# Cross attention and two gated layers on one core: the state reads' softmax moves into the x reads' stage, and both halves of the attention get new places

## The chip, the core and the metric

The kernel runs on one core of a Trainium2 chip: TensorE (PE) multiplies 128-row tiles into PSUM, VectorE (DVE), ScalarE (ACT) and GpSimd (POOL) work on tiles, and SyncE (SP) issues nearly all DMAs from one queue. Every engine takes its instructions in a fixed order. The metric is the device time in microseconds (us) of one execution; a version's time is the median of its runs.

## What is computed

```python
B, H, S, Ns, D = 8, 8, 512, 32, 64
a  = softmax(x @ state.T / 8)        # x reads:     [B, H, S, Ns]
a2 = softmax(state @ x.T / 8)        # state reads: [B, H, Ns, S]
attn = concat([a @ state, a2 @ x], axis=2)     # per head
t = attn.transpose(0, 2, 1, 3).reshape(8 * 544, 512)
t = (sigmoid(t @ w_gate) * (t @ w_val)) @ w_out        # d_ff 1536
out = square(relu(t @ w_in)) @ w_out2                  # d_ff 2048
```

Both softmaxes come from the same scores: `a2` is the softmax over the other axis. Everything is fp32; a product is made of three matmuls of split operands (high by high, high by low, low by high; lines 182 to 184). The weights arrive as 64-bit words that are converted on the way (`to_single`, line 108).

## The kernel before

**First part.** The gated layer's products with w_gate and w_val are taken with the state first: `state_weights` (L457) multiplies the 32 state rows of each head by a chunk of w_gate and w_val and stores the result in DRAM (`g_dram`, tile `gd`), for blocks 0 to 3 and then for 4 to 7. There are six chunks of 256 columns. The x rows of a block then need only their attention weights `a`: `front_x` makes the gate (`psg`), its sigmoid `sg`, the value (`psv`) and their product `g` (L556) from `a` and `gg`, the split form of a chunk's part `gi` that `load_g` fetched from `gd`. `back1` multiplies `g` by w_out1 into four accumulators. One front and one back are a **unit**: blocks 0 to 3 with f = 0 to 5 (units 0 to 23), again with f = 6 to 11 (24 to 47), then blocks 4 to 7 with 12 each (48 to 95). Unit 58, for one, is block 4 with f = 10: the first that needs chunk 5 for blocks 4 to 7. Units 96 to 107 are the state rows of all blocks (`front_s`): their input `xs_t` is the state reads of all eight blocks, split into high and low in `split_states`, their weights `ws` come back from DRAM (`load_gv`).

**Attention.** Block b has two groups g of four heads. Stage A (`LX, A20, A21, A3, A4`) loads x transposed, makes the scores `s2`, stores them to DRAM (`s_dram`, tile `sd`) and makes the x reads' weights `a` from their transpose `e1`, with an exponential on ScalarE (L336). Stage B (`LN, LS, B4, B5, SX, B60, B61, B7`) loads x and the scores (`e2`), takes the exponential with its sum (L359), scales by the reciprocal (L363 on ScalarE for blocks 0 to 3, else L365 on VectorE), transposes (`ps_e2`, `et`), multiplies by the split x (`xs`; `ps_sr`, `tmp`, `sw`) and turns the result into `xs_t` (`ps_so`). ScalarE holds one table of functions: between a sigmoid and an exponential stands an ACT_TABLE_LOAD.

**Beside it** w_in2 and w_out2 are converted and written back in the form of the second part (`prep_steps`: loads `raw`, tiles `c`, `wa`, `wu`, stores `wi` and `wo`).

**What sets the order.** Each stage is a closure that `spread` puts at a due time counted in units; `front_x`, `front_s` and `back1` run what is due at their six steps. From the program so written a scheduler makes the fixed order of each engine; it may move an instruction ahead of others of its engine. The small PSUM tiles of the attention, of `state_weights` and of the transposes (tag `at`) share a ring of two and get their slots in the order of the program. Where a tile's slot or its data are late, all behind it in its engine's order wait. The pools `e2`, `s2`, `xs`, `et` have one buffer each.

**Second part** (from unit 107 on): the squared-relu layer with seven products for each two by two blocks.

In the trace's names digits at a word's end are left out: `e` is `e1` or `e2`, `s` is `s2`, `ps_s` is `ps_s2`.

Of the kernel before, what the change touches and what calls it, by code (L numbers as in the profile page):

```python
# [32 lines left out]
def kernel(  # L33
# [247 lines left out]

    def group_stages(b, g):

        v = {}
# [37 lines left out]

        def a4():
# [22 lines left out]
            nc.vector.tensor_sub(out=a[:, 1, g, :], in0=a1, in1=a[:, 0, g, :].bitcast(F32))  # L346

        def ls():
            v["e2"] = f_p.tile([P, S], F32, tag="e2", name="e2", bufs=1)
            nc.sync.dma_start(out=v["e2"], in_=s_dram[b, g])  # L350

        def b4():

            s2 = v.pop("e2")
            nm = sm_p.tile([P, 1], F32, tag="nm", name="nm")
            sm = sm_p.tile([P, 1], F32, tag="sum", name="sum")
            nc.vector.tensor_reduce(out=nm, in_=s2, axis=AX.X, op=ALU.max, negate=True)
            nc.vector.tensor_scalar_mul(nm, nm, scale)
            nc.scalar.activation(out=s2, in_=s2, func=AF.Exp, bias=nm, scale=scale, accum_out=sm)  # L359
            nc.vector.tensor_scalar_add(sm, sm, 1e-9)  # L360
            nc.vector.reciprocal(out=sm, in_=sm)
# [80 lines left out]
    def attention(b):
        gs = [group_stages(b, g) for g in range(2)]
        pick = lambda names: [
            (lambda: None) if n == "-" else gs[int(n[-1])][n[:-2]] for n in names
        ]
        return [lambda: prep_diag(b), *pick(ORDER_A)], pick(ORDER_B)
# [114 lines left out]
    def split_states():  # L562
        t = two["sp"].tile([P, 2, KD, NSTATE], F32R, name="sp")
        nc.scalar.copy(out=t[:, 0], in_=xs_t)
        nc.vector.tensor_sub(out=t[:, 1], in0=xs_t, in1=t[:, 0].bitcast(F32))
        s_parts["a"] = t
# [543 lines left out]
```

## Time and profile before

| | us |
|---|---|
| median of 3 runs (1497.92 to 1499.72) | 1499.65 |
| the profiled execution's own time | 1500.54 |
| its span, first to last instruction | 1498.8 |
| PE busy | 1431.0 (95%) |
| DVE, ACT, POOL busy | 940.2, 748.8, 246.0 |
| DMA | 311.68 MB, mean 208 GB/s |

A matmul's record is longer than its share of a busy PE, since matmuls overlap; the number of matmuls in a window tells more than the busy time. The first part, with attention, takes about the first 790 us, the second the rest.

### The profile page before, as it was taken

To read this page: it belongs to the slowest core of one execution; us is meant where nothing else is said; L and a number is where in the kernel's file an instruction comes from. 1 tells how busy PE (TensorE), PEld (TensorE's weight loads), DVE (VectorE), ACT (ScalarE), POOL (GpSimd) and SP (SyncE) were. 2 spreads that over 40 slices of the span, in tenths; PEclk is the share of its full clock that TensorE was granted. 3 is DMA by queue.
4 is the path that set the end of the run, shared out by engine and by line. 5 is a ranking of instruction groups with operands and counts; after the bars stand their busy time and mean duration, and the time that the engine had idled before them with its cause. 6 is when DMAs were issued, how large, how long until landed. Compare 5 with 4: busy or idle time off the path is not lost.

```text
span 1498.8 us, 19379 instructions
## 1 busy us (share of the span) xinstructions
PE 1431.0 (95%) x6552; PEld 1176.9 (79%) x6552; DVE 940.2 (63%) x1579; ACT 748.8 (50%) x1291; POOL 246.0 (16%) x216
## 2 busy tenths in 40 slices
PE   5879999999999989999899999999999999999998
PEld 3558878887787677888798788888888888888887
DVE  7986887578889987555536655734575356433443
ACT  6865876456678887666424522332242223232211
POOL 1112213232344544333101100000000000000000
PEclk9889999999999999999999999999999999999999
DMA  9984799699999864333677844644365443645442
GB/s 265 341 263 120 229 328 339 210 363 292 323 296 286 254 211 145 95 113 92 242 271 250 274 158 147 217 146 143 133 227 188 151 152 134 222 124 195 155 145 80
DMA packets 244595, 311.68 MB, mean 208 GB/s; under 512 B 105361, under 2 KB 152977, under 8 KB 244497
## 3 DMA queue, kind: packets, MB, share of 16 engines
q1 hardware_dynamic: 242224, 309.66, 63.8%
q10 hardware_dynamic: 2272, 0.79, 0.3%
q8 instruction: 52, 0.85, 0.2%
q14 instruction: 47, 0.38, 0.1%
HBM read 221.25 MB, written 89.13 MB: 207 GB/s over the span
## 4 chain that ended last, share of the span: by engine, by line
PE 72%; DVE 10%; ACT 7%; DMA 7%; issue 3%; SPq 1%; POOL 0%; ACTq 0%; DVEq 0%; POOLq 0%
PE o L182 8%; PE o L183 8%; PE o L184 8%; PE px L183 4%; PE px L182 4%; PE px L184 4%; PE acc L183 4%; PE acc L184 3%; PE acc L182 3%; DMA raw<-in_moe_w_out_dram 2%; PE psg L182 2%; PE psg L183 2%; PE psg L184 2%; PE psv L182 2%; PE psv L183 2%
## 5 line engine op out<-in xcount | busy, mean ns | idle before, releaser
L182 PE MATMUL o<-wo,g2h 128*128 128x512 f32 x512 | 198.6, 390 | 3.7 <-DMA wo<-wo 3.0
L183 PE MATMUL o<-wo,g2h 128*128 128x512 f32 x512 | 199.1, 389 | 0.0
L184 PE MATMUL o<-wo,g2l 128*128 128x512 f32 x512 | 193.9, 389 | 0.0
L537 POOL TENSOR_TENSOR gg<-gi,gg 128x512 fp32r<-128x512 f32 x96 | 135.3, 1412 | 350.5 <-ACT gg L536 284.2
L183 PE MATMUL acc<-gl,o 128*128 128x512 f32 (+1 forms) x432 | 164.4, 381 | 3.7 <-DVE gl L190 3.7
L184 PE MATMUL acc<-gh,o 128*128 128x512 f32 (+1 forms) x432 | 163.0, 378 | 0.0
L841 ACT CAST g2h<-c 128x512 fp32r<-128x512 f32 x96 | 59.3, 622 | 178.8 <-DVE c L837 178.8
L182 PE MATMUL acc<-gh,o 128*128 128x512 f32 (+1 forms) x432 | 139.3, 380 | 0.6 <-DVE y L624 0.4
L893 DVE TENSOR_TENSOR y<-o,y 128x512 f32<-128x512 f32 x102 | 68.5, 688 | 103.5 <-PE o L184 102.8
L182 PEld LDWEIGHTS o<-wo,g2h 128*128 128x128 f32 x512 | 96.1, 188 | 24.9 <-ACT p L826 3.0
L184 PEld LDWEIGHTS o<-wo,g2l 128*128 128x128 f32 x512 | 96.1, 188 | 19.8
L183 PEld LDWEIGHTS o<-wo,g2h 128*128 128x128 f32 x512 | 96.2, 188 | 19.5
L190 DVE TENSOR_TENSOR gl<-g,gh 128x512 fp32r<-128x512 f32 (+1 forms) x108 | 88.4, 818 | 36.3 <-ACT gh L189 35.8
L182 PE MATMUL px<-xh,wi 128*128 128x512 f32 x256 | 99.8, 390 | 0.0
L183 PE MATMUL px<-xl,wi 128*128 128x512 f32 x256 | 99.7, 389 | 0.0
L184 PE MATMUL px<-xh,wi 128*128 128x512 f32 x256 | 99.6, 389 | 0.0
L183 PEld LDWEIGHTS acc<-gl,o 128*128 128x128 f32 x432 | 81.3, 188 | 21.3 <-DVE gl L190 6.9
L182 PEld LDWEIGHTS acc<-gh,o 128*128 128x128 f32 x432 | 80.6, 189 | 17.4 <-DVE y L624 1.1
L184 PEld LDWEIGHTS acc<-gh,o 128*128 128x128 f32 x432 | 81.3, 188 | 14.6
L182 PE MATMUL psg<-a,gg 128*128 128x512 f32 x192 | 78.6, 409 | 14.8 <-ACT sg L550 12.1
L556 DVE TENSOR_TENSOR g<-psv,sg 128x512 f32<-128x512 f32 x96 | 65.6, 683 | 35.4 <-PE psv L184 21.6
L189 ACT CAST gh<-g 128x512 fp32r<-128x512 f32 (+1 forms) x108 | 64.3, 596 | 40.4 <-DVE g L556 23.0
(188 smaller groups left out, 3268.7 us busy)
## 6 DMA issues: line engine op xcount, KB each, us to landing
wi<-wi SPq DMA_DIRECT2D x256, 256.0 KB, 3.1
wo<-wo SPq DMA_DIRECT2D x64, 512.0 KB, 5.5
gd<-go SPq DMA_DIRECT2D x192, 128.0 KB, 4.4
gi<-gd SPq DMA_DIRECT2D x96, 256.0 KB, 4.0
wi<-wa SPq DMA_DIRECT2D x32, 512.0 KB, 5.0
wd<-w SPq DMA_DIRECT2D x24, 512.0 KB, 5.1
ws<-wd SPq DMA_DIRECT2D x24, 512.0 KB, 6.7
raw<-in_moe_w_out_dram SPq DMA_DIRECT2D x20, 512.0 KB, 6.2
```

The lines of the kernel that those rows point to most:

```text
L182: nc.tensor.matmul(ps, lh, rh, start=start, stop=False, skip_group_check=more)
L183: nc.tensor.matmul(ps, lh, rl, start=False, stop=False, skip_group_check=more)
L184: nc.tensor.matmul(ps, ll, rh, start=False, stop=stop, skip_group_check=more)
L189: nc.scalar.copy(out=gh[:, :n], in_=g32[:, :n])
L190: nc.vector.tensor_sub(out=gl[:, :n], in0=g32[:, :n], in1=gh[:, :n].bitcast(F32))
L537: nc.gpsimd.tensor_sub(out=t[:, 1], in0=src, in1=t[:, 0].bitcast(F32))
L556: nc.vector.tensor_mul(out=g32, in0=ps, in1=sg)
L841: nc.scalar.copy(out=h, in_=c)
L893: nc.vector.tensor_add(out=y, in0=acc, in1=y)
```

## The change

Stage B's exponential goes. For blocks 2 to 7 (`own`) A4 itself makes the state reads' weights from `s2`, right beside the exponential of `e1`, scales them on VectorE and stores the weights in place of the scores; B only loads them. For blocks 0 and 1, A4 still stores scores; they are loaded again (`LS`) and the A4 of block 4 or 5 (`pair`) takes their exponential with its own two. The scaling on ScalarE is gone. `A` of block 4 and `B` of block 0 are one list of stages (`ORDER_AB`), as are 5 and 1; the due times of all other stages are new, and the prep steps are spread evenly from 30.6 to 91. The splits of x^T (`xt`, high and low in one tile) and of x (`xs`) share one ring of three buffers; the raw state shares the buffer of `e2`. `xs_t` is split in two halves.

```diff
-    xx_p = att.enter_context(tc.tile_pool(name="xx", bufs=2))
+    xx_p = att.enter_context(tc.tile_pool(name="xx", bufs=3))
...
-        raw = f_p.tile([P, DM], F32, tag="xs", name="sraw", bufs=1)
+        raw = f_p.tile([P, DM], F32, tag="e2", name="sraw", bufs=1)
...
+    LATE = 2
+    e2_tiles = {}
...
-                h = xx_p.tile([P, S], F32R, tag="xth", name="xth")
-                l = xx_p.tile([P, S], F32R, tag="xtl", name="xtl")
+                t = xx_p.tile([P, 2, S], F32R, tag="xx", name="xt")
+                h, l = t[:, 0, :], t[:, 1, :]
...
+        own, pair = b >= LATE, b - QB if b - QB in range(LATE) else None
...
+            rows = [s2] if own else []
+            if pair is not None:
+                rows.append(e2_tiles[pair, g])
             nc.vector.transpose(flat, s2)
-            nc.sync.dma_start(out=s_dram[b, g], in_=s2)
+            if not own:
+                nc.sync.dma_start(out=s_dram[b, g], in_=s2)
+            small = []
+            for t in rows:
...
+                nc.vector.tensor_reduce(out=nm, in_=t, axis=AX.X, op=ALU.max, negate=True)
+                nc.vector.tensor_scalar_mul(nm, nm, scale)
+                small.append((t, nm, sm))
...
             nc.scalar.activation(out=e1, in_=e1, func=AF.Exp, scale=scale)
+            for t, nm, sm in small:
+                nc.scalar.activation(out=t, in_=t, func=AF.Exp, bias=nm, scale=scale, accum_out=sm)
...
+            for t, nm, sm in small:
+                nc.vector.tensor_scalar_add(sm, sm, 1e-9)
+                nc.vector.reciprocal(out=sm, in_=sm)
+                nc.vector.tensor_scalar_mul(t, t, sm)
+            if own:
+                nc.sync.dma_start(out=s_dram[b, g], in_=s2)
...
-        def b4():
...
-            if busy:
-                nc.scalar.activation(out=s2, in_=s2, func=AF.Copy, scale=sm)
-            else:
-                nc.vector.tensor_scalar_mul(s2, s2, sm)
...
-                xs = f_p.tile([P, 2, 2, NT, D], F32R, tag="xs", name="xs", bufs=1)
+                xs = xx_p.tile([P, 2, 2, NT, D], F32R, tag="xx", name="xs")
...
-    for b in range(QB, B):
-        start = 33 + 7 * (b - QB)
-        spread(att_a[b], start, start + 7)
-    for b in range(B):
-        start = 45 + 5 * b
-        spread(att_b[b], start, start + 5.4)
+    for b in range(LATE):
+        start = 31 + 9.5 * b
+        spread(att_both(QB + b), start, start + 9.5)
+    for b in range(QB + LATE, B):
+        start = 52 + 10 * (b - QB - LATE)
+        spread(att_first(b), start, start + 8)
+    for b in range(LATE, B):
+        start = 50.5 + 7 * (b - LATE)
+        spread(att_second(b), start, start + 7)
...
-    spread([split_states], u_s - 0.55, u_s)
+    for g in range(2):
+        spread([lambda g=g: split_states(g)], u_s - 0.55, u_s)
...
-    spread(prep[: len(prep) * 3 // 5], 30.6, 58)
-    spread(prep[len(prep) * 3 // 5 :], 58, 90)
+    spread(prep, 30.6, 91)
```

ScalarE in the second third of the first part, before, around an exponential of a B (L359) and one of an A (L336), with the sigmoid of a unit between them:

```order
L359 ACT_TABLE_LOAD
L359 ACTIVATE e2_5144,sum_5237<-e2_5144,nm_5236 128x512
L550 ACT_TABLE_LOAD
L550 ACTIVATE sg_5778<-psg_5771 128x512
L118 ACTIVATE c_6934<-raw_6883 128x512
L536 CAST gg_5855<-gi_5751 128x512
L336 ACT_TABLE_LOAD
L336 ACTIVATE e1_5244<-e1_5244 128x512
```

and of the changed kernel around an A4 of block 5, which takes block 1's along:

```order
L352 ACT_TABLE_LOAD
L352 ACTIVATE s2_4021,sum_4095<-s2_4021,nm_4094 128x512
L352 ACTIVATE e2_3909,sum_4099<-e2_3909,nm_4098 128x512
L350 ACTIVATE e1_4089<-e1_4089 128x512
L493 COPY go_4047<-ps_g_4039 128x512
L563 CAST gg_4513<-gi_4363 128x512
L189 CAST gh_4414<-g32_4407 128x512
L577 ACT_TABLE_LOAD
L577 ACTIVATE sg_4492<-psg_4485 128x512
```

Three exponentials now follow one table load. All in all 56 table loads stand in the order before and 30 in the order after.

SP's queue ahead of the load of unit 58 (`gi`, the last row), before:

```order
L699 DMA wi4_218<-wa_5132 128x1024
L106 DMA raw_5563<-in_moe2_w_in_dram 128x4x256
L478 DMA gd4_5_151<-go_4622 32x2x512
L478 DMA gd5_5_157<-go_4622 32x2x512
L478 DMA gd6_5_163<-go_4622 32x2x512
L478 DMA gd7_5_169<-go_4622 32x2x512
L699 DMA wi4_218<-wa_5211 128x1024
L106 DMA raw_5695<-in_moe2_w_out_dram 128x1024
L529 DMA gi_5058<-gd4_5_151 128x2x256
```

and after:

```order
L106 DMA raw_5889<-in_moe2_w_in_dram 128x4x256
L372 DMA e2_4839<-sd2_1_199 128x512
L505 DMA gd4_5_151<-go_4680 32x2x512
L505 DMA gd5_5_157<-go_4680 32x2x512
L505 DMA gd6_5_163<-go_4680 32x2x512
L505 DMA gd7_5_169<-go_4680 32x2x512
L713 DMA wo3_225<-wu_5397 128x1024
L106 DMA raw_6042<-in_moe2_w_in_dram 128x4x256
L726 DMA wi4_218<-wa_5611 128x1024
L556 DMA gi_5026<-gd4_5_151 128x2x256
```

The last four stores of chunk 5 (`gd4` to `gd7`) stand a few rows ahead of the load both times. Between the loads of units 57 and 58 there are 18 other DMAs before and 41 after: all four groups of chunk 5's stores, nine loads of raw weights, and loads of stages A and B.

PE at the first unit of the state rows (`psg<-sp,ws`), before:

```order
L183 MATMUL acc3_7138<-gl_7568,o11_2468 128x512
L184 MATMUL acc3_7138<-gh_7567,o11_2468 128x512
L398 MATMUL ps_sr_7079<-xs_7058,et_7008 128x256 x4
L420 MATMUL ps_so_7113<-ident_117,sw_7038 128x128
L182 MATMUL psg_7599<-sp_7553,ws_7577 128x256
```

and after:

```order
L182 MATMUL acc3_7011<-gh_7538,o11_2484 128x512
L182 MATMUL psg_7570<-sp0_7521,ws_7548 128x256
L183 MATMUL psg_7570<-sp0_7521,ws_7548 128x256
L184 MATMUL psg_7570<-sp0_7521,ws_7548 128x256
L182 MATMUL psv_7585<-sp0_7521,ws_7548 128x256
```

The last product and transpose of block 7's state reads stood right ahead of the state rows; now they stand at units 90 and 91, and the state rows begin within the back of unit 95.

## Rows read from the trace of the kernel before

**Rows 1.** The page: busy time of PE, and its slices of 37.5 us.

```profile
PE 1431.0 (95%) x6552; PEld 1176.9 (79%) x6552; DVE 940.2 (63%) x1579; ACT 748.8 (50%) x1291; POOL 246.0 (16%) x216
PE   5879999999999989999899999999999999999998
DMA  9984799699999864333677844644365443645442
```

**Rows 2.** Windows: an untroubled one, then nine between openings of units.

```profile
core 0: us, PE busy (x) PEld busy (x) DVE busy (x) ACT busy (x) POOL busy (x), PEclk, DMA share, GB/s
875.00:900.00 25.00, 25.00 (x112) 20.69 (x111) 15.63 (x25) 6.46 (x11) 0.00 (x0) 1.00 0.49 168
237.60:311.50 73.90, 73.26 (x323) 60.09 (x322) 43.52 (x64) 34.97 (x62) 22.91 (x21) 1.00 0.84 279
311.50:384.10 72.60, 70.58 (x310) 57.78 (x309) 59.44 (x91) 46.13 (x74) 25.09 (x24) 1.00 0.96 314
384.10:453.00 68.90, 67.72 (x309) 55.64 (x308) 56.52 (x100) 51.60 (x86) 25.71 (x22) 1.00 1.00 308
453.00:475.70 22.70, 20.22 (x88) 15.42 (x87) 21.73 (x37) 18.13 (x32) 9.87 (x8) 1.00 0.91 295
475.70:490.50 14.80, 14.56 (x58) 11.47 (x59) 13.97 (x25) 13.69 (x24) 10.19 (x12) 0.88 1.09 292
490.50:589.10 98.60, 87.58 (x382) 67.41 (x381) 83.41 (x147) 79.13 (x133) 44.60 (x34) 0.98 0.65 202
589.10:720.40 131.30, 131.30 (x625) 109.79 (x624) 74.70 (x143) 89.10 (x156) 48.82 (x37) 1.00 0.37 103
720.40:743.90 23.50, 17.99 (x86) 15.47 (x85) 12.93 (x26) 10.82 (x23) 2.65 (x2) 0.85 0.83 298
743.90:766.80 22.90, 22.90 (x187) 22.63 (x186) 10.59 (x21) 8.21 (x18) 0.00 (x0) 1.00 0.89 322
```

**Rows 3.** Waits of PE over the span: total us, times, longest.

```profile
PE psg L182 <- ACT sg L550: 12.1, 13, 3.0
```

**Rows 4.** Groups of ACT by shape: busy us, mean ns, idle before.

```profile
L550 ACT ACT_TABLE_LOAD x28 | 35.9, 1283 | 2.2 <-PE psg L184 1.7
...
L363 ACT ACTIVATE e<-e,sum 128x512 f32<-128x512 f32 x8 | 5.8, 721 | 0.0
```

**Rows 5.** Groups of DVE by shape: the same scaling there.

```profile
L365 DVE TENSOR_SCALAR e<-e,sum 128x512 f32<-128x512 f32 x8 | 4.7, 584 | 0.3
```

**Rows 6.** Timeline of ACT at one table load: start, us, instruction.

```profile
511.97 0.59 ACT L307 CAST xth<-xf 128x512 fp32r<-128x512 f32 x1
512.58 1.28 ACT L550 ACT_TABLE_LOAD   x1
513.87 0.60 ACT L550 ACTIVATE sg<-psg 128x512 f32<-128x512 f32 x1
```

**Rows 7.** Timeline of SP: the issues of gi for units 57 and 58.

```profile
448.32 0.37 SPq L529 DMA_DIRECT2D gi<-gd  x1
...
468.26 1.61 SPq L529 DMA_DIRECT2D gi<-gd  x2
```

**Rows 8.** Timeline of PE: the openings of units 57 and 58.

```profile
467.07 0.50 PE L182 MATMUL psg<-a,gg 128*128 128x512 f32 x1 [0.38 <-ACT sg L550]
...
475.74 0.50 PE L182 MATMUL psg<-a,gg 128*128 128x512 f32 x1 [1.30 <-ACT gg L536]
```

**Rows 9.** Timeline of PE: the state rows begin.

```profile
735.87 0.48 PE L182 MATMUL psg<-sp,ws 128*128 128x256 f32 x1 [3.32 <-ACT sp L564]
```

**Rows 10.** SP's issue of the first eight ws, and their times to landing.

```profile
724.29 3.84 SPq L570 DMA_DIRECT2D ws<-wd  x8
...
DMA to landing us min/median/max: 3.4/7.8/10.6
```

More of the change, by code (lines that the diff above doesn't have):

```diff
@@ L280 @@
     a_tiles = {}
+    LATE = 2
+    e2_tiles = {}
     def group_stages(b, g):
         v = {}
-        busy = b < QB
         by_pe = b < NPE
@@ L331, in a4 @@
             s2 = v.pop("s2")
+            rows = [s2] if own else []
+            if pair is not None:
+                rows.append(e2_tiles[pair, g])
             nc.vector.transpose(flat, s2)
-            nc.sync.dma_start(out=s_dram[b, g], in_=s2)
+            if not own:
+                nc.sync.dma_start(out=s_dram[b, g], in_=s2)
+            small = []
+            for t in rows:
+                nm = sm_p.tile([P, 1], F32, tag="nm", name="nm")
+                sm = sm_p.tile([P, 1], F32, tag="sum", name="sum")
+                nc.vector.tensor_reduce(out=nm, in_=t, axis=AX.X, op=ALU.max, negate=True)
+                nc.vector.tensor_scalar_mul(nm, nm, scale)
+                small.append((t, nm, sm))
             nc.vector.tensor_reduce(out=m1, in_=e1, axis=AX.X, op=ALU.max)
@@ L346, in a4 @@
             nc.vector.tensor_sub(out=a[:, 1, g, :], in0=a1, in1=a[:, 0, g, :].bitcast(F32))
-        def ls():
-            v["e2"] = f_p.tile([P, S], F32, tag="e2", name="e2", bufs=1)
-            nc.sync.dma_start(out=v["e2"], in_=s_dram[b, g])
-        def b4():
[L354 to L361, printed above, removed]
-            if busy:
-                nc.scalar.activation(out=s2, in_=s2, func=AF.Copy, scale=sm)
-            else:
-                nc.vector.tensor_scalar_mul(s2, s2, sm)
-            v["e2"] = s2
+            for t, nm, sm in small:
[4 more added lines that the diff above has]
+                nc.sync.dma_start(out=s_dram[b, g], in_=s2)
+        def ls():
+            t = f_p.tile([P, S], F32, tag="e2", name="e2", bufs=1)
+            nc.sync.dma_start(out=t, in_=s_dram[b, g])
+            e2_tiles[b, g] = t
         def b5():
-            e2 = v.pop("e2")
+            e2 = e2_tiles.pop((b, g))
             ps = at_p.tile([P, 512], F32, tag="at", name="ps_e2")
@@ L431, in group_stages @@
             "LX": lx, "LN": ln, "LS": ls, "A20": a2(0), "A21": a2(1), "A3": a3, "A4": a4, "SX0": sx(0), "SX1": sx(1),
-            "B4": b4, "B5": b5, "B60": b6(0), "B61": b6(1), "B7": b7,
+            "B5": b5, "B60": b6(0), "B61": b6(1), "B7": b7,
         }
@@ L437, with pick, att_first, att_second @@
     ORDER_B = (
-        "LN.0 LS.0 - - - B4.0 SX0.0 - B5.0 LS.1 - B60.0 SX1.0 LN.1 - B61.0 B4.1 SX0.1 - B5.1 "
-        "B7.0 - B60.1 SX1.1 - B61.1 - B7.1"
+        "LN.0 LS.0 - - B5.0 SX0.0 SX1.0 LN.1 LS.1 - B60.0 B61.0 - B5.1 SX0.1 SX1.1 "
+        "B7.0 - B60.1 B61.1 - B7.1"
     ).split()
[L442 to L447, printed above, removed]
+    ORDER_AB = (
+        "LX.0 LN.0 LS.0 - A20.0 A21.0 LX.1 A3.0 SX0.0 SX1.0 A4.0 - B5.0 LN.1 LS.1 A20.1 B60.0 B61.0 "
+        "A21.1 A3.1 SX0.1 SX1.1 B7.0 A4.1 - B5.1 - B60.1 B61.1 - B7.1"
+    ).split()
+    stages = {(b, g): group_stages(b, g) for b in range(B) for g in range(2)}
+    def pick(names, ba, bb):
+        fns = []
+        for n in names:
+            key, _, g = n.partition(".")
+            if n == "-":
+                fns.append(lambda: None)
+            else:
+                b = ba if key in ("LX", "A20", "A21", "A3", "A4") else bb
+                fns.append(stages[b, int(g)][key])
+        return fns
+    def att_first(b):
+        return [lambda: prep_diag(b), *pick(ORDER_A, b, b)]
+    def att_second(b):
+        return pick(ORDER_B, b, b)
+    def att_both(b):
+        return [lambda: prep_diag(b), *pick(ORDER_AB, b, b - QB)]
     w1 = {}
@@ L560, with split_states @@
     s_parts = {}
[L562 to L566, printed above, removed]
+    def split_states(g):
+        t = two["sp"].tile([P, 2, 2, NSTATE], F32R, name=f"sp{g}")
+        src = xs_t[:, 2 * g : 2 * g + 2, :]
+        nc.scalar.copy(out=t[:, 0], in_=src)
+        nc.vector.tensor_sub(out=t[:, 1], in0=src, in1=t[:, 0].bitcast(F32))
+        s_parts[g] = t
     def load_gv(ch, c):
@@ L575, in front_s @@
         n = NSTATE
-        t = s_parts["a"]
         out_ps = []
@@ L956 @@
     raw = load_states(0)
-    att_a, att_b = {}, {}
-    for b in range(B):
-        att_a[b], att_b[b] = attention(b)
     steps0 = chunk_steps(0, 0, [0, 1])
-    a0 = att_a[0]
+    a0 = att_first(0)
     steps0.pop(0)()
@@ L979 @@
     spread(chunk_steps(2, 0, outs[2]), 1.2, 3)
-    spread(att_a[1], 1, 4)
-    spread(att_a[2], 4, 8)
-    spread(att_a[3], 8, 12)
+    spread(att_first(1), 1, 4)
+    spread(att_first(2), 4, 8)
+    spread(att_first(3), 8, 12)
     for ch in range(3, NCH):
```

3 lines of the change are left out of this document (1 added, 2 removed).

## The prediction

> **What bounds the kernel now.** I read the page first, then the windows at unit openings, the waits of PE, and the order of SP's queue against the timeline. The profiled execution took 1500.54 us, its span 1498.8, so 1.7 us lie outside it; it is 0.9 us above the median of 1499.65. PE is busy 95% of the span [rows 1], and the untroubled stretch shows a 512-column matmul each 25/112 = 0.2232 us [rows 2]. Half of that for 256 columns and 0.109 us for a 128-column transpose give every stretch a floor, from the matmuls that the order lists. The change edits nothing behind unit 101, where both orders are alike again.
>
> A unit "opens" at its first gate matmul (psg). Nine stretches between openings run from 237.6 to 766.8 us [rows 2]; I call them S1 (units 24 to 34), S2 (35 to 44), S3 (45 to 54), S4 (55 to 57), S5 (58, 59), S6 (60 to 72), S7 (73 to 94), S8 (95, 96), S9 (97 to 101). Their lengths are 73.9, 72.6, 68.9, 22.7, 14.8, 98.6, 131.3, 23.5 and 22.9 us, their floors 71.6, 69.0, 65.8, 18.5, 12.3, 78.5, 128.5, 14.0 and 21.4. S7 has nothing in PE's way and runs at 1.022 of its floor; I use that as the pace. So the loss is small in S1 to S3, 4 us in S4, 2 in S5, 18 in S6, 9 in S8. In S4 VectorE is busy 21.7 of 22.7 us, in S6 83.4 of 98.6 beside ScalarE's 79.1 [rows 2]. The longest wait of PE is for the sigmoid of ScalarE [rows 3], and a read of the state's softmax stands before several of those sigmoids with a table load of its own. DMA is saturated in S2 and S3 (0.96 and 1.00, 308 to 314 GB/s) [rows 2], yet PE loses little there, as gi is fetched early.
>
> **The change, part by part.**
> *Exponentials.* 56 table loads become 30. A load is 1.28 us [rows 4], so ScalarE sheds 33.4 us, and 8 scalings of 0.72 us go to VectorE at 0.58 us each (4.7 us) [rows 4, 5]. Of those loads 12 stood in S6 and 8 stand there now: 5.1 us less in front of sigmoids. The rest lay in S7, where ScalarE is busy 89 of 131 us and nobody waits: worth nothing there. In the trace a load costs its own duration: the cast ends at 512.56, the load starts at 512.58 and the sigmoid at 513.87 [rows 6]. The Trainium skill (ScalarE: Activation LUTs, What ACT_TABLE_LOAD costs) adds a drain of 1.38 us to every switch; by it S6 would shed 10.6 us instead of 5.1 and my sum would be 5 us lower. No such pause stands in these rows, so the sum goes by 1.28.
>
> *Where the work now stands.* No matmul is added. The order puts the matmuls of the second halves of blocks 0 and 1 into units 36 to 58. The floors become 72.8, 65.1, 68.2, 26.5, 5.5, 82.0, 126.6, 10.7 and 22.8 us.
>
> S1 to S3: VectorE's instructions go from 254 to 273 over 215.4 us, 0.59 us each by S2's row (59.44/91 and 56.52/100 in S3), thus under 170 us of work: PE sets the time. I give S1 its old 2.3 us over the floor (75.1), S2 66.5 at pace and 0.8, S3 69.7 and 0.6: **212.7** against 215.4. Below, pace alone: 210.6; above, the old 215.4.
>
> *The hole ahead of unit 58.* Unit 58 is the first that reads chunk 5 of blocks 4 to 7. All small PSUM tiles share a ring of two in the order of the program, and the last product of chunk 5 stands in it behind the end of block 1's second half. That half waits for its scores, the joint exponentials, a transpose and two sums. A late link is thus late for chunk 5. The order shows the result: between the gates of units 57 and 58 VectorE has 48 instructions where it had 16, ScalarE 39 where it had 14, PE 14.2 us of matmuls where it had 6.0, and on SP's queue 41 DMAs (12.6 MB) stand between the gi of 57 and of 58 where 18 (6.0 MB) stood.
> From three sides: PE alone 14.5 us. VectorE, 48 instructions at 13.97/25 to 83.41/147 us, 0.567 [rows 2]: 27.2 us, and S4 shows that it can be that full. The queue: before, the two gi were issued 19.9 us apart [rows 7] for 6.29 MB with the load itself; 12.85 MB at that rate are 40.7 us. The gi of 57 was issued 18.7 us ahead of its unit and that of 58 7.5 us, with PE waiting 1.30 us for its split [rows 7, 8]. With the same lead the opening of 58 comes 40.7 - 18.7 + 7.5 = 29.5 us after that of 57; with no lead beyond 7.5, 40.7. I take **32**, near the queue's lower figure, since the rows before gi 57 are light, with a little for SP standing behind producers (the splits of w_in2). With 12.5 us for units 55 and 56, S4 is **44.5** against 22.7. SP, VectorE and ScalarE are all queued behind here: gi 58 behind the stores of wi and wo, sigmoid 58 behind the pair of exponentials.
> S5: VectorE 20 instructions at 0.559 [rows 2], **11.2** against 14.8, PE 5.6.
> S6: VectorE 151 instructions at 0.567 = 85.7, PE 82.0 x 1.022 = 83.8, ScalarE about the same count as before (127 against 125) with four loads less. Before, the length stood 98.6 - 83.4 = 15.2 us above VectorE's work. Lower end 85.7, upper end 100.9. I take 15.2 - 5.1 for the loads and another 1 for half as many bursts: **95.0**.
> S7: 126.6 x 1.022 = **129.4**.
>
> *The end of the attention.* Before, PE finished block 7's second half in S8, waited 3.32 us for the split of xs_t [rows 9], and the clock was at 1.2 GHz (mean 0.85) in part of it [rows 2]. Now that half ends by unit 91 and the split is two instructions of half size. But ws is fetched only when unit 95's front has released its tiles, at 724.29 us before [rows 10]; eight come in the order of chunks 0 and 1 by turns, so unit 96 needs the seventh. They land 3.4 to 10.6 us after their issues, which spread over 3.8 us [rows 10]; the eighth lands some 14 us after the first issue and the seventh about 12.5. What replaces the wait for xs_t is thus the wait for ws: 2.8 us of unit 95's front, 12.5, 0.7 of matmuls and 0.5 for the clock, **16.5** against 23.5. Ends: 15 if the clock holds, 18.5 if it falls for long. S9 gets six products of the second part earlier than before: 22.9 + 1.4 = **24.3**.
> The ring of three and the state tile moved into tag e2 only change who waits for a slot: nothing by themselves, and what they force is in the order above. The start (0 to 237.6 us, DMA at nine tenths or more in the first two slices of 37.5 us [rows 1]) loses one early read (four small VectorE instructions) and gets block 2's: 0, from -2 to +2.
>
> **Sum.** 212.7 + 44.5 + 11.2 + 95.0 + 129.4 + 16.5 + 24.3 = 533.6 against 529.2: +4.4, so 1504.9 for this execution and 1504 against the median.
>
> **Rivals.**
> *The hole costs only VectorE's share and the lighter ScalarE frees S6: faster.* The place is the opening of 58, the point is the queue: if gi 58 lands before VectorE is through, the hole is 27.2. With S6 at 88 and S8 at 15.5 the sum is 212.7 + 39.7 + 11.2 + 88 + 129.4 + 15.5 + 24.3 = 520.8, -8.4: 1491. For it: half the table loads go, and S4's row shows VectorE full without a large loss. Against: 12.6 MB ahead of one load.
> *SP's queue is served one by one: much slower.* gi 58 has no lead, the hole is 40.7, and S6 keeps its old overhead (100.9): 548.2, +19: 1519. For it: 41 DMAs that wait for splits of VectorE, ScalarE and POOL in turn. Against: units 53 to 56 leave SP little to do.
> *The stretches balance:* hole 30 and S6 93 give +0.4, 1500. It is the lower part of my case, no mechanism of its own.
>
> **How the numbers follow.** The forecast with its own range of 1497 to 1511 has 0.48, the faster rival 0.31, the slower 0.21. About 0.2% (3 us) is what a measurement of this kernel can tell from no change. My case lies half within that bound (0.22), hardly under it (0.01), else above (0.25); the faster rival gives 0.28 faster and 0.03 same; the slower one 0.21. Faster 0.29, same 0.25, slower 0.46. The range 1491 to 1519 takes in both rivals' centres and leaves their outer halves.
>
> **What would show it.** In the profile after: units 57 and 58 open some 32 us apart with PE idle for 15 us or more and a DMA share near 1 there; under 28 us refutes the queue's part, 40 confirms the slower rival. S6 must be shorter than 98.6 with fewer waits for sg; if it is not, table loads were not what held PE. In S8 PE should wait for ws, not for sp. I am wrong if chunk 5 is ready in time after all, or if S1 to S3 lose several us to the joint exponentials, which I put at nearly nothing.

## The result, and the profile of the changed kernel

The changed kernel takes 1517.7 us in the median of six runs (1514.93 to 1522.94) against 1499.49; the ratio is 1.0126 with an interval of 1.0107 to 1.0145: slower. The profiled execution has a span of 1513.1 against 1498.8 us and is the fastest of its six (1514.93), so the stages below account for 14 of the 18 us.

The page after, busy time and slices of PE and DMA, which answer to [rows 1]:

```profile
PE 1433.6 (95%) x6552; PEld 1177.2 (78%) x6552; DVE 949.1 (63%) x1588; ACT 709.6 (47%) x1258; POOL 248.0 (16%) x216
...
PE   5869999999997898999899999999999999999998
...
DMA  9984799798989786432586844645356443635442
```

One slice of PE, the thirteenth (454 to 492 us), has fallen to 7. The windows of after are cut at the same openings of units as those of [rows 2], but S4 is cut once more, at unit 57: S1, S2, S3, units 55 and 56, unit 57 (from its opening to that of 58), S5, S6, S7, S8, S9.

```profile
core 0: us, PE busy (x) PEld busy (x) DVE busy (x) ACT busy (x) POOL busy (x), PEclk, DMA share, GB/s
235.10:309.00 73.90, 73.90 (x330) 61.21 (x329) 46.20 (x75) 39.29 (x70) 21.05 (x19) 1.00 0.90 308
309.00:379.60 70.60, 68.00 (x307) 54.85 (x305) 55.31 (x99) 42.00 (x76) 23.50 (x22) 1.00 0.90 266
379.60:451.10 71.50, 70.50 (x314) 57.47 (x315) 53.47 (x100) 43.48 (x80) 26.34 (x23) 1.00 0.87 269
451.10:466.70 15.60, 13.38 (x61) 10.22 (x59) 13.41 (x22) 10.32 (x19) 5.96 (x4) 1.00 0.86 267
466.70:495.40 28.70, 19.64 (x78) 15.14 (x78) 21.26 (x42) 17.61 (x34) 8.95 (x10) 0.77 0.99 312
495.40:506.90 11.50, 7.87 (x26) 5.75 (x26) 10.84 (x24) 10.14 (x18) 6.25 (x5) 0.84 0.92 290
506.90:607.30 100.40, 90.97 (x394) 71.05 (x392) 95.35 (x151) 68.55 (x125) 51.63 (x42) 0.97 0.72 223
607.30:740.00 132.70, 130.60 (x607) 107.63 (x608) 76.36 (x122) 70.93 (x134) 44.30 (x33) 1.00 0.35 102
740.00:756.60 16.60, 12.66 (x62) 10.14 (x60) 3.88 (x6) 3.80 (x7) 0.00 (x0) 0.95 0.77 276
756.60:781.90 25.30, 25.30 (x194) 24.79 (x194) 4.97 (x12) 4.36 (x11) 0.00 (x0) 0.96 0.84 305
```

Two rows matter. Unit 57 lasts 28.7 us where it lasted 8.7 [rows 8], with PE busy 19.64 of them, the DMA share at 0.99 and the granted clock down to a mean of 0.77. And in S6 VectorE is busy 95.35 of 100.4 us, where it was busy 83.41 of 98.6 before [rows 2].

**The gap.** SP's queue in the timeline, the issues of gi for units 57 and 58 ([rows 7] before):

```profile
446.57 0.36 SPq L556 DMA_DIRECT2D gi<-gd  x1
...
487.82 1.46 SPq L556 DMA_DIRECT2D gi<-gd  x2
```

and PE there: the opening of 57, the last product of chunk 5 (`ps_g`), what of the attention stands behind it, and the opening of 58:

```profile
466.67 0.49 PE L182 MATMUL psg<-a,gg 128*128 128x512 f32 x1 [1.10 <-ACT sg L577]
...
478.04 0.39 PE L184 MATMUL ps_g<-wagain,st_t 128*128 128x512 f32 x1
...
481.69 1.82 PE L405 MATMUL ps_sr<-xs,et 128*128 128x256 f32 x8 [2.82 <-DVE et L384]
487.14 1.08 PE L380 MATMUL ps_e<-ident,e 128*128 128x128 f32 x4 [3.64 <-DMA e<-sd]
489.13 0.45 PE L427 MATMUL ps_so<-ident,sw 128*128 128x128 f32 x1 [0.91 <-DVE sw L418]
...
493.24 2.34 PE L405 MATMUL ps_sr<-xs,et 128*128 128x256 f32 x8
495.37 0.57 PE L182 MATMUL psg<-a,gg 128*128 128x512 f32 x1
```

and ScalarE's first cast of gi for unit 58:

```profile
494.60 0.62 ACT L563 CAST gg<-gi 128x512 fp32r<-128x512 f32 x1
```

The two loads are issued 41.2 us apart, and with the second load itself that is 12.8 MB: 3.21 us a MB, close to the 19.9 us for 6.3 MB before. The load of 57 has a lead of 20.1 us on its unit, that of 58 of 7.5: 41.2 - 20.1 + 7.5 = 28.6. These are three parts of one length, not a proof that the queue sets it. Beside it PE works through block 1's second half, nearly every step of which waits for another engine or for a load in the full queue. ScalarE's first cast of gi ends at 495.2, and PE's last work of block 1 at 495.6: both chains end within a microsecond, so neither alone can be called the bound. The time a MB takes in the queue is no constant: in the other runs with a gap the two issues stood 33.8 us apart for 9.2 MB (e2, below), 30.8 for 8.9 (e3), 49.8 for 13.4 (e8) and 36.7 for 10.2 (e10), 3.5 to 3.7 us a MB.

**S8.** PE's waits in units 95 and 96 are for ws, as foreseen; a wait for sp ([rows 9]) is no longer there:

```profile
PE psg L182 <- DMA ws<-wd: 3.9, 3, 1.6
```

### The profile page after: what moved, and what is told of

Its sections match the earlier page's. It is cut to its first block, busy times and chain, and to the rows that moved or that the text cites. A ratio compares the mean times of both kernels' runs of the same rounds, so it can differ in the third digit from the quotient of the medians.

```text
span 1513.1 us, 19388 instructions
## 1 busy us (share of the span) xinstructions
PE 1433.6 (95%) x6552; PEld 1177.2 (78%) x6552; DVE 949.1 (63%) x1588; ACT 709.6 (47%) x1258; POOL 248.0 (16%) x216
## 4 chain that ended last, share of the span: by engine, by line
PE 72%; DVE 10%; DMA 6%; ACT 5%; issue 4%; POOL 1%; SPq 1%; DVEq 0%; ACTq 0%; POOLq 0%
PE o L182 8%; PE o L183 8%; PE o L184 8%; PE px L182 4%; PE acc L183 4%; PE px L183 4%; PE px L184 4%; PE acc L184 4%; PE acc L182 4%; PE psg L182 2%; PE psv L182 2%; PE psg L183 2%; PE psg L184 2%; PE psv L184 2%; PE psv L183 2%
## 5 line engine op out<-in xcount | busy, mean ns | idle before, releaser
L184 PE MATMUL acc<-gh,o 128*128 128x512 f32 (+1 forms) x432 | 164.3, 380 | 0.0
L182 PE MATMUL acc<-gh,o 128*128 128x512 f32 (+1 forms) x432 | 141.4, 382 | 3.6 <-ACT gh L189 2.9
L190 DVE TENSOR_TENSOR gl<-g,gh 128x512 fp32r<-128x512 f32 (+1 forms) x108 | 90.6, 839 | 27.1 <-ACT gh L189 26.4
L189 ACT CAST gh<-g 128x512 fp32r<-128x512 f32 (+1 forms) x108 | 64.3, 595 | 42.8 <-DVE g L583 24.7
```

Source lines behind the costliest of these rows:

```text
L182: nc.tensor.matmul(ps, lh, rh, start=start, stop=False, skip_group_check=more)
L184: nc.tensor.matmul(ps, ll, rh, start=False, stop=stop, skip_group_check=more)
L189: nc.scalar.copy(out=gh[:, :n], in_=g32[:, :n])
L190: nc.vector.tensor_sub(out=gl[:, :n], in0=g32[:, :n], in1=gh[:, :n].bitcast(F32))
```

## All runs by stage

Lengths between openings of units, in us, of each profiled execution. "Lost" is the sum over units 24 to 101 less PE's floor, counted as in the prediction (479 to 480 us in all of them). The last columns are the median of the timed runs and the ratio to the kernel before, which was timed anew beside each group of runs (medians 1498.6 to 1500.0). The stages are those of one execution each. The order of e9 differs from that of the kernel before by table loads only, and S2, where both traces have five of them, takes 74.3 us in it instead of 72.7: a difference of 2 us in a stage tells little.

| run | S1 to S3 | 55, 56 | 57 | S5 | S6 | S7 | S8 | S9 | sum | lost | median | ratio |
|---|---|---|---|---|---|---|---|---|---|---|---|---|
| before | 215.5 | 14.0 | 8.7 | 14.8 | 98.6 | 131.4 | 23.4 | 23.0 | 529.3 | 49.5 | 1499.5 | |
| after | 216.1 | 15.5 | 28.7 | 11.6 | 100.4 | 132.7 | 16.5 | 25.3 | 546.8 | 66.6 | 1517.7 | 1.0126 |
| e1 | 222.9 | 13.3 | 6.6 | 12.5 | 100.7 | 134.6 | 17.3 | 24.5 | 532.4 | 52.2 | 1502.8 | 1.0025 |
| e2 | 217.3 | 13.2 | 20.9 | 14.0 | 91.4 | 132.3 | 20.3 | 23.0 | 532.6 | 52.3 | 1504.7 | 1.0032 |
| e3 | 230.5 | 14.8 | 20.6 | 9.8 | 96.6 | 133.0 | 16.6 | 26.9 | 548.7 | 68.9 | 1518.1 | 1.0116 |
| e4 | 222.9 | 13.8 | 8.1 | 12.3 | 98.3 | 137.5 | 17.3 | 26.2 | 536.3 | 56.1 | 1503.2 | 1.0014 |
| e5 | 216.5 | 14.1 | 8.1 | 14.3 | 93.3 | 134.6 | 23.8 | 23.0 | 527.6 | 47.8 | 1499.1 | 0.9999 |
| e6 | 221.4 | 15.0 | 7.1 | 16.1 | 93.5 | 132.3 | 25.3 | 23.0 | 533.8 | 53.6 | 1508.3 | 1.0072 |
| e7 | 222.0 | 12.6 | 6.0 | 15.9 | 95.1 | 133.9 | 17.7 | 24.0 | 527.2 | 48.3 | 1505.0 | 1.0045 |
| e8 | 215.1 | 12.8 | 41.3 | 13.8 | 92.7 | 131.0 | 16.0 | 26.4 | 549.1 | 68.9 | 1519.2 | 1.0143 |
| e9 | 217.3 | 14.1 | 8.5 | 14.2 | 92.1 | 131.4 | 23.6 | 23.0 | 524.1 | 44.3 | 1493.8 | 0.9957 |
| e10 | 216.1 | 15.0 | 26.2 | 14.5 | 94.7 | 133.7 | 17.7 | 25.4 | 543.4 | 63.1 | 1511.6 | 1.0077 |
| e11 | 216.8 | 17.2 | 6.6 | 16.2 | 97.7 | 141.6 | 17.9 | 25.9 | 540.0 | 59.8 | 1509.5 | 1.0064 |
| e12 | 220.7 | 17.0 | 8.2 | 15.5 | 94.9 | 135.0 | 17.4 | 25.9 | 534.7 | 54.5 | 1505.2 | 1.0033 |

Of the 17.1 us that the changed kernel loses beyond the kernel before, units 55 to 59 hold all: their floors are 30.9 and 32.0 us, their lengths 37.5 and 55.8, so 6.6 us of loss have become 23.8. The other stages together lose 42.8 us, against 42.9. What the change does outside the gap, good and bad, cancels.

## The experiments

**The place of chunk 5's products.** In e1 one pair of numbers of the changed kernel differs:

```diff
-        spread(chunk_steps(ch, 1, []), 24.5 + 4.5 * ch, 29 + 4.5 * ch)
+        spread(chunk_steps(ch, 1, []), 24.5 + 4.0 * ch, 28.5 + 4.0 * ch)
```

> The changed kernel with one number changed: the second pass of the chunks is due every 4.0 units instead of 4.5, so the last product of chunk 5 stands ahead of the end of block 1's second half. In its order 8 VectorE instructions and 11 DMAs (3.7 MB) stand between units 57 and 58 where the changed kernel has 48 and 42 (12.8 MB). Theory (the place of chunk 5's products makes the loss): units 57 and 58 open 8 to 10 us apart instead of 28.7, units 55 to 59 take 38 instead of 55.8 us, units 60 to 72 stay at 100 to 103; in all 1497 to 1502 us. Rival (the work is the bound, SP's queue and VectorE are merely full at one place or at another): what is saved there comes back in units 60 to 72, which get 161 VectorE instructions instead of 151 (110 us or more); in all 1509 to 1516.

It took 1502.8 us, ratio to before 1.0025 (1.0011 to 1.0038): 14.9 us less than the changed kernel. The windows of unit 57 and of S6 in e1, columns as above:

```profile
472.10:478.70 6.60, 6.51 (x30) 5.14 (x31) 6.54 (x12) 4.57 (x9) 3.34 (x3) 1.00 0.92 155
491.20:591.90 100.70, 86.94 (x382) 66.00 (x380) 93.56 (x159) 74.68 (x133) 49.19 (x45) 1.00 0.80 246
```

The gap is gone and S6 is as long as it was. Of the 22.1 us that unit 57 gave back, S1 to S3 took 6.8. The place theory holds; the time is 0.8 us above its range.

Is an earlier chunk worth that much by itself? e5 makes the same edit in the kernel before.

> The kernel before with the second pass of the chunks due every 4.0 units instead of 4.5, nothing else. In its order 13 VectorE instructions and 4 DMAs (1.8 MB) stand between units 57 and 58 where it had 16 and 19 (6.3 MB). Theory (the earlier chunks only help where a burst stood ahead of unit 58): 57 to 58 takes 6.5 us instead of 8.7, units 60 to 72 with 143 instead of 138 VectorE instructions 99 to 102; in all 1497 to 1502 us. Rival (earlier chunks are worth 15 us by themselves, whatever stood ahead of unit 58): 1484 to 1490.

1499.05 us, 0.9999 (0.9987 to 1.0010): nothing. S6 became 5.3 us shorter and S7 and S1 to S3 4.2 longer. So the 15 us of e1 belong to the gap.

e10 and e11 move chunk 5 alone in the changed kernel, by 1.5 and 2.5 units:

```diff
     for ch in range(NCH):
-        spread(chunk_steps(ch, 1, []), 24.5 + 4.5 * ch, 29 + 4.5 * ch)
+        early = 0 if ch < NCH - 1 else 2.5
+        spread(chunk_steps(ch, 1, []), 24.5 + 4.5 * ch - early, 29 + 4.5 * ch - early)
```

> The changed kernel with chunk 5 alone, the last, due 1.5 units earlier. Units 24 to 44 have the same numbers of instructions as in the changed kernel; between units 57 and 58 stand 37 VectorE instructions and 31 DMAs (10.2 MB) instead of 48 and 42 (12.8 MB). Theory (the gap is what stands between, by the queue at 3.2 us a MB, less the leads of 20.1 and 7.5 us that the changed kernel shows): units 57 and 58 open 20 us apart instead of 28.7, in all 1507 to 1512. Rival (any work that is taken out of the gap comes back behind it): gap 20, units 58 to 72 120 us or more instead of 112, in all 1515 to 1519.

> The same with chunk 5 alone due 2.5 units earlier: 6 VectorE instructions and 18 DMAs (5.5 MB) stand between units 57 and 58. Theory (as in e10): the gap is 7 us, bounded by the matmuls; units 60 to 72 with 155 VectorE instructions 98 to 102; units 35 to 54 stay at 142; in all 1497 to 1503. Rival (the work comes back behind it): units 58 to 72 130 us or more, in all 1510 or more.

e10 took 1511.6 us, within the theory's bounds, but by luck: its gap is 26.2 and not 20, since the two gi were issued 36.7 us apart for 10.2 MB, 3.6 us a MB. What it gained lies in S6 (94.7 us instead of 100.4), on which the theory said nothing. e11 took 1509.5, missing both theories. Unit 57, S6 and S7 of e11:

```profile
470.80:477.40 6.60, 6.60 (x34) 5.59 (x32) 6.38 (x13) 5.50 (x11) 1.54 (x2) 0.97 0.98 329
493.60:591.30 97.70, 81.94 (x363) 64.06 (x361) 86.88 (x152) 72.80 (x127) 49.03 (x41) 0.98 0.79 236
591.30:733.00 141.70, 138.40 (x635) 113.84 (x636) 93.28 (x151) 77.93 (x152) 54.52 (x41) 0.98 0.40 121
```

The gap is closed as in e1, yet the median fell by 8.2 and not 14.9 us: S7 is 8.9 us longer than in the changed kernel (VectorE 93.28 us of work there instead of 76.36), units 55 to 59 without 57 another 6.3. Part of this is PE's own work, which stands in other stages now: PE's floor in S7 is 131.1 us in e11's trace and 126.6 in the changed kernel's. What is lost above the floor grows by 4.4 us in S7 and by 4.4 in S6 (97.7 us over a floor of 74.9, where the changed kernel has 100.4 over 82.0). In the gap VectorE had done 21.26 us of work while PE waited, and without it that work has to be done elsewhere; but that it is VectorE's work which holds PE is argued and only in part shown: in S6 and S7 together PE's waits for VectorE rise from 9.4 to 12.6 us, and those for ScalarE's sigmoid from 2.0 to 6.1. So closing the gap is worth 8 to 15 us here, by what stands behind it. Why e1 gives back less than e11 no run tells.

**The exponentials alone, and the times alone.** e2 puts the new exponentials of blocks 2 to 7 into the kernel before, with its times and rings:

```diff
             nc.vector.transpose(flat, s2)
-            nc.sync.dma_start(out=s_dram[b, g], in_=s2)
+            if own:
...
+            else:
+                nc.sync.dma_start(out=s_dram[b, g], in_=s2)
...
             nc.scalar.activation(out=e1, in_=e1, func=AF.Exp, scale=scale)
+            if own:
+                nc.scalar.activation(out=s2, in_=s2, func=AF.Exp, bias=nm, scale=scale, accum_out=sm)
```

> The kernel before with the exponentials alone: for blocks 2 to 7 A4 makes the weights of the state reads beside its own exponential and stores them, B4 does nothing there; blocks 0 and 1, all due times, rings and the split of the states as before. 36 table loads instead of 56, 4 instead of 12 of them in units 60 to 72. Its order also has 33 VectorE instructions and 26 DMAs (9.2 MB) between units 57 and 58 where the kernel before has 16 and 19 (6.3 MB). Theory (burst): 9.2 MB are 29.5 us of the queue, with the leads of before the openings of 57 and 58 come 18 us apart (8.6 before), +10; units 60 to 72 shed 5 to 8 us by fewer loads and 128 instead of 138 VectorE instructions; in all 1501 to 1506 us. Rival (the exponentials' new place does nothing but shed loads): 1490 to 1495. Second rival (the loads never held PE): units 60 to 72 keep 98 us, in all 1509.

1504.7 us, 1.0032 (1.0015 to 1.0049), within the first theory; the gap was to be 18 us. Unit 57 and S6 of e2:

```profile
470.10:491.00 20.90, 14.42 (x55) 10.19 (x53) 18.53 (x41) 16.98 (x30) 4.51 (x6) 0.84 0.87 287
505.10:596.50 91.40, 86.29 (x387) 68.85 (x385) 81.88 (x143) 63.52 (x118) 44.27 (x33) 0.98 0.68 206
```

S6 sheds 7.2 us, and a gap of 20.9 us opens ahead of unit 58 although no due time was changed: in the order that the scheduler makes of it, 33 VectorE instructions stand between units 57 and 58 instead of 16.

e6 closes that gap by earlier chunks, as e1 did.

> e2_exponentials_alone with the chunks due every 4.0 units: 16 VectorE instructions and 5 DMAs (1.8 MB) between units 57 and 58 instead of 33 and 26. Theory (burst, with VectorE as the bound behind it): 57 to 58 takes 6.5 us instead of 20.9, -14; units 60 to 72 get 146 VectorE instructions instead of 128, 96 to 98 us instead of 91.4, +5; units 45 to 54 with 114 instead of 100 VectorE instructions +2; in all 1496 to 1500. Rival (the gap is gone and nothing is given back): 1489 to 1492. Second rival (all is given back): 1503 to 1506.

1508.3 us, 1.0072 (1.0049 to 1.0094): the first theory is wrong, and it came out above even the second rival. 13.8 us went out of unit 57 and came back elsewhere: S1 to S3 +4.1, units 55 and 56 +1.8, S5 and S6 +2.1 each, S8 +5.0, where block 7's second half ends 14.4 us after the opening of unit 95 instead of 8.7. The gap is thus no loss that can be taken off by itself; from this base it was worth nothing.

e3 is the counterpart, the kernel before with the new due times:

```diff
-    for b in range(QB, B):
-        start = 33 + 7 * (b - QB)
-        spread(att_a[b], start, start + 7)
...
+    for b in range(2):
+        start = 31 + 9.5 * b
+        spread(att_a[QB + b], start, start + 9.5)
+        spread(att_b[b], start, start + 9.5)
...
-    spread(prep[: len(prep) * 3 // 5], 30.6, 58)
-    spread(prep[len(prep) * 3 // 5 :], 58, 90)
+    spread(prep, 30.6, 91)
```

> The kernel before with the changed kernel's due times alone: block 0's and 1's second halves beside the first halves of blocks 4 and 5 from 31 and 40.5 on, the rest as in the changed kernel, the prep steps even; exponentials, rings and the split of the states as before, 54 table loads. Between units 57 and 58 stand 25 VectorE instructions and 30 DMAs (8.9 MB). Theory (burst): the openings of 57 and 58 come 17 us apart, +9; units 95 and 96 take some 17 instead of 23.5, as the second halves end at unit 94, -6; units 60 to 72 have 147 VectorE instructions and 10 loads, 100 us; in all 1502 to 1507. Rival (the times alone make the whole loss of the changed kernel, whatever the number of instructions between 57 and 58): 1514 to 1519.

1518.1 us, 1.0116 (1.0098 to 1.0134): the rival's figure. Units 57 and 58 open 20.6 us apart, which is 12 more than before where the theory had 9; the rest lies in S2 and S3, which the theory had overlooked:

```profile
310.10:387.50 77.40, 71.90 (x314) 57.65 (x314) 56.21 (x97) 50.09 (x84) 25.47 (x24) 0.98 0.83 260
387.50:466.90 79.40, 74.25 (x323) 57.06 (x321) 55.33 (x93) 50.85 (x85) 24.90 (x23) 1.00 0.88 268
```

156.8 us against 142.1 in the changed kernel, with VectorE's work the same (111.5 and 108.8 us) and ScalarE's 15.5 us more (100.9 and 85.5; 14 table loads in units 35 to 54 of its order and 6 of the changed kernel's). Does the changed kernel fit block 0's and 1's second halves in there by its joint exponentials, or by the new ring? e8 gives the changed kernel the old rings:

```diff
-    xx_p = att.enter_context(tc.tile_pool(name="xx", bufs=3))
+    xx_p = att.enter_context(tc.tile_pool(name="xx", bufs=2))
...
-                t = xx_p.tile([P, 2, S], F32R, tag="xx", name="xt")
-                h, l = t[:, 0, :], t[:, 1, :]
+                h = xx_p.tile([P, S], F32R, tag="xth", name="xth")
+                l = xx_p.tile([P, S], F32R, tag="xtl", name="xtl")
...
-                xs = xx_p.tile([P, 2, 2, NT, D], F32R, tag="xx", name="xs")
+                xs = f_p.tile([P, 2, 2, NT, D], F32R, tag="xs", name="xs", bufs=1)
```

> The changed kernel with the rings of the kernel before: high and low of split x transposed in two rings of two, split x in one buffer of its own. Its order has 58 VectorE instructions and 44 DMAs (13.4 MB) between units 57 and 58, 134 instead of 151 VectorE instructions in units 60 to 72. Theory (the ring of three does nothing by itself; units 35 to 54 take 142 us in the changed kernel and 157 in e3_times_alone because of the exponentials, 6 table loads there instead of 14): units 35 to 54 stay at 140 to 146, 57 to 58 takes 30 us by the queue, units 60 to 72 some 93; in all 1511 to 1518. Rival (the ring of three is what keeps units 35 to 54 short): these take 150 to 157 us, in all 1522 or more.

1519.2 us, 1.0143 (1.0123 to 1.0162), 1.2 us above the theory's range. S2 and S3 take 140.4, so the rival is refuted: the ring does nothing there. What is left are the exponentials and the merged list of stages, which e3 has not; these two were not parted. But the gap is 41.3 us where the theory had 30, and one row of PE's waits in it (total, times, longest) tells what the ring does:

```profile
PE ps_sr L405 <- POOL xs L394: 9.0, 2, 6.9
```

With one buffer for split x, PE waits for it twice in the gap; S6 gives 7.7 of the 12.6 us back (92.7 against 100.4).

**Table loads.** e9 is the kernel before with `func=AF.Sigmoid` in the place of `AF.Exp` in b4: the state reads' exponential is left out so that its loads go and nothing else moves.

> The kernel before with a sigmoid in the place of the exponential of the state reads (the second softmax is left out in this way): the order of every engine is the same row for row, but for 32 table loads fewer (24 instead of 56; 4 instead of 12 in units 60 to 72, none instead of 16 in 73 to 94, 2 instead of 8 in 45 to 57). Theory of the prediction (loads ahead of sigmoids hold PE in units 60 to 72): these take 92 to 95 us instead of 98.6, in all 1492 to 1496 us. Rival (VectorE and the chains of the attention hold PE there, the loads lie beside them): 97 to 99 us, in all 1497 to 1500.

1493.8 us, 0.9957 (0.9942 to 0.9972): faster. The trace has 26 table loads (the expectation counted 24): 6 instead of 14 in the time of S6, none instead of 16 in S7. S6 and S7 of e9, and PE's first wait in S6:

```profile
489.70:581.80 92.10, 85.44 (x381) 66.17 (x380) 83.69 (x148) 70.34 (x126) 45.41 (x36) 1.00 0.72 224
581.80:713.20 131.40, 131.40 (x625) 109.84 (x624) 74.28 (x143) 67.79 (x140) 48.99 (x37) 1.00 0.38 103
```

```profile
PE psg L182 <- ACT sg L550: 1.7, 2, 1.1
```

Eight loads fewer shorten S6 by 6.5 us, 0.81 us each of the 1.283 that one lasts; sixteen fewer in S7 change nothing (131.4 both times). The Trainium skill (ScalarE: Activation LUTs, What ACT_TABLE_LOAD costs) gives 2.66 us for a switch with its drain; eight of these would be an estimated 21 us, and this run shows under a third of it.

**Attempts at a faster version.** e4 is e1 with the prep steps due as in the kernel before.

> As e1_chunks_early, and the prep steps due as in the kernel before: three fifths by unit 58. Its order has 150 VectorE instructions in units 60 to 72 instead of e1's 161, 23 instead of 19 in 58 and 59, 145 instead of 134 in 45 to 57. Theory (VectorE bounds units 60 to 72): these take 6 to 8 us less than in e1, in all 4 to 8 us less than e1. Rival (chains of the attention bound them, not VectorE's amount of work): within 2 us of e1.

1503.2 us, 1.0014 (1.0000 to 1.0028), within 2 us of e1, as the rival had it: S6 is 2.4 us shorter instead of 6 to 8, S7 2.9 longer. VectorE's amount of work does not by itself set S6. e7 and e12 give all eight blocks their exponentials in A4 (`LATE = 0`), with the first halves and the prep at the old times, the second halves 5.5 units apart from 45 on, and e1's chunks or chunk 5 alone.

> The changed kernel with its A4 taking the state reads' exponentials of all eight blocks at once (no block stores scores, no block's second half stands beside another's first), the due times of the kernel before for the first halves and the prep steps, second halves from unit 45 on at 5.5 units each, chunks every 4.0 units. Between units 57 and 58 stand 10 VectorE instructions and 3 DMAs; units 60 to 72 have 139 VectorE instructions; the second halves end at unit 91; units 0 to 23 have 9 VectorE instructions more than in e6. Theory (the burst ahead of unit 58 and VectorE in units 60 to 72 make the loss, the early end of the second halves is a gain of 5 to 7): units 60 to 72 take 94 to 97 us, 95 and 96 take 17, units 35 to 54 some 142; in all 1488 to 1494. Rival (more exponentials ahead of unit 24 cost what the rest saves): units 0 to 23 are 5 us longer, in all 1497 or more.

> As e7_all_own_chunks, but of the chunks only chunk 5 moved (2.5 units earlier) and the second halves due from 45 on at 5.5 units. 92 VectorE instructions in units 45 to 54 (e7: 106), 10 between 57 and 58, 139 in units 60 to 72; the order behind unit 107 is that of the kernel before again (e7's ScalarE order differed there, and its second part took 716.0 us instead of 710). Theory (burst, VectorE in units 60 to 72, early end of the attention): units 24 to 101 take 522 to 527 us, the second part 709 to 711, in all 1491 to 1497. Rival (what is taken from one stage stands in another): 24 to 101 take 529 or more, in all 1499 or more.

1505.0 us (1.0045, 1.0029 to 1.0062) and 1505.2 (1.0033, 1.0020 to 1.0047): both theories miss. e12 fits its rival (what is taken from one stage stands in another). e7 has the time of its rival but not the cause, since unit 24 opens at 237.1 us in it, no later than before (237.6). e7's units 24 to 101 are 2.1 us shorter than before, but what follows is 5.7 longer, with PE waiting 4.1 us for one wo. e12 has the old second part, and loses more in S1 to S3, units 55 and 56, S7 and S9 than S6 and S8 gain. No version with all its work beats the kernel before.

## Why the prediction was right or wrong

It said 1504, with a range of 1491 to 1519, and 0.46 for slower. The time lies in the range, 1.3 us under its upper end, and on the likeliest side; the size was off by 14 us (18 us slower instead of 4), 10 of them in the terms and most of the rest in the profiled execution being the fastest of its six.

| term | forecast | profile after |
|---|---|---|
| S1 to S3 | 212.7 | 216.1 |
| S4, with the gap | 44.5 (32) | 44.2 (28.7) |
| S5 | 11.2 | 11.6 |
| S6 | 95.0 | 100.4 |
| S7 | 129.4 | 132.7 |
| S8 | 16.5 | 16.5 |
| S9 | 24.3 | 25.3 |
| start to unit 24 | 0 (-2 to +2) | -2.5 |

- **The gap** was right in place and size, and in the pile of work ahead of chunk 5's last stores: e1 and e11 take the pile away and the gap goes. With 10.2 instead of 12.8 MB it is only 2.5 us shorter (e10), and which of the two chains in it sets its length stays open. The low figure of the queue, 29.5, was nearer than the 32 that I took. The slower rival had the time (1519) and S6 (100.9), but its gap of 40.7 was 12 us too long: the load of 57 kept its longer lead, 20.1 us against 7.5.
- **S6 is the term that failed**, 5.4 us too small. Its part on the loads came out near its size, by two errors that cancel. The sum had four loads fewer at 1.28 us each, 5.1 us, counted in the order. In the time of S6 the traces have 14 before and 7 after, and e9 prices a load there at 0.81 us, together 5.7. ScalarE's table loads in S6 before:

```profile
L550 ACT ACT_TABLE_LOAD x7 | 9.0, 1283 | 0.1
...
L359 ACT ACT_TABLE_LOAD x4 | 5.1, 1283 | 0.5 <-issue 0.4
...
L336 ACT ACT_TABLE_LOAD x3 | 3.8, 1283 | 0.1
```

  and after:

```profile
L352 ACT ACT_TABLE_LOAD x3 | 3.8, 1283 | 1.5 <-DVE nm L346 1.4
L577 ACT ACT_TABLE_LOAD x3 | 3.8, 1283 | 0.1
...
L350 ACT ACT_TABLE_LOAD x1 | 1.3, 1283 | 0.0
```

  What was too small is VectorE's work. The lower end of S6, VectorE's 151 instructions at the 0.567 us of [rows 2], was 85.7 us; the row has 95.35 for 151, 0.631 each, and S6 lies 5 us above that. That VectorE sets the length of S6 is not shown, however: e11, with VectorE busy 8.5 us less there than in the changed kernel (86.88), is 2.7 us shorter in S6, and e4, with 4.2 less than e1 (89.37 and 93.56), 2.4.
- My own test for S6 ("if it is not shorter, table loads were not what held PE") was a bad one. S6 is not shorter, but the waits for sg fell as they should. PE's first three waits in S6 after, total, times and longest; the kernel before had 6.2 us in 5 waits for sg there:

```profile
PE acc L183 <- DVE gl L190: 3.5, 4, 1.9
PE psv L182 <- DVE g L583: 2.8, 3, 1.8
PE psg L182 <- ACT sg L577: 1.7, 1, 1.7
```

  The longest waits have changed their releaser, from ScalarE to VectorE. e9, with the same order as the kernel before but for the loads, separates what the test could not.
- **S1 to S3** were to gain 2.7 us, at pace in S2 and S3. They lose 10.0 us against 9.1 before, and S2 is 3.3 us over its forecast of 67.3: 70.6 us over a floor of 65.1. The pace taken from S7 was too kind there. Why, no run shows: VectorE, at 78 and 75% in S2 and S3, is less busy than the 82% before, and PE's waits in the two come to 3.5 us together. The prediction also misread a row: VectorE's mean in S2 before is 59.44/91 = 0.653 us and not 0.59, which changes nothing in its sum.
- **S7** was put at pace and is 3.3 us over it; at its start PE still waits for VectorE (1.6 us for one `g` at 610). e11, where VectorE has 93.28 us to do in S7, loses 10.5 there against 6.1.
- **S8**, the wait for ws in the place of that for xs_t, and "worth nothing" for the loads in S7 were right (e9). The joint exponentials in S2 and S3, at which I put nearly nothing, stand beside a larger figure: e3, without them and at the same times, takes 14.7 us more there. How much of that is theirs and how much that of the merged list of stages was not parted.

## What to carry to other kernels

When instructions pile up ahead of one load in an in-order queue, the gap can be estimated from the order: bytes between the two loads by the queue's rate (3.2 to 3.7 us a MB here), less the lead of the first load and plus that of the second. At 3.2 us a MB the estimates for e2, e3, e10 and e8 came out 3 to 11 us too short. But a gap in one engine is time in which the others work; before counting its removal as a gain, ask which engine would have to do that work elsewhere (here 22 us of gap were worth 15 or 8, and 14 us of it from another base nothing). And when a wait is shortened in a stage where a second engine is at 85%, look at that engine's instructions next: they need not keep the mean of the old row when more stands beside them. The busy time of that engine is still not the length of the stage, as e4 and e11 show.
